# Cosine attention and a gated product on one core: pair 0's turned half copied earlier, the first tile of the second product parted at pass 12, one unit's loads behind a gather

## The chip, the cores and the metric

One Trainium2 chip, of which the kernel uses one core. The metric is the device time of one execution in microseconds (us), the median over several runs. Engines are named as in the profile: PE (TensorE, the matmuls), ACT (ScalarE), DVE (VectorE), POOL (GpSimd, which also issues the loads that convert f32 to bf16) and SP (SyncE, which here only issues DMAs).

## The reference

Inputs are q, k, v of 8 batches x 12 heads x 448 rows x 64 columns, and two weight matrices, 768 x 2048 and 2048 x 768. Cut to what is computed:

```
q_n = q / |q|;  k_n = k / |k|                      # along the 64 columns
attn = softmax(q_n @ k_n.T / 0.1)                  # 448 x 448 for each head
x    = (attn @ v) as a 3584 x 768 matrix           # rows: batch and row, columns: head and column
h    = x @ w_in;  g = h * cos(h)                   # 3584 x 2048
out  = g @ w_out                                   # 3584 x 768
```

## The kernel before, in words

**Pieces of work.** Two heads are a pair; 48 pairs are numbered 0 to 47, six to a batch. Three pairs are a unit; units 0 to 15, two to a batch. One batch's x is 448 columns of `xT`.

**What a pair goes through.** SP loads its k and q into `raw` (`load`, L586, DMAs at L589). They are squared (`square`, L618, on ACT at L627 or POOL at L629), DVE sums the squares (`reduce`, L632, L636), ACT turns the sum into a reciprocal root with a logarithm and an exponential (`rnorm`, L644, L657 and L660; for some units POOL does it, L653 and L654), and POOL or DVE scales q and k into `qks` (`scale`, L663, L668). `transposes` (L681) turns `qks` into `qkT`: for pairs 0 to 8 on PE (L692) with a DVE copy out of PSUM (L706), from pair 9 on by a transposing DMA of SP (L685). Pair 0 alone is handled in two parts a and b: four of the seven row blocks, then three; each has its own scaling, transposes and copy, and the two copies go from two PSUM tiles, `MP` and `AV`. `scores` (L709) makes four score blocks (block 0 is half as wide, L727; blocks 1 to 3, L719), each followed by ACT's exponential into `PX` (L734). Blocks alternate between PSUM banks, so a block also waits for whoever read the bank last. `attend` (L739) multiplies with v: R (the short block, L760), AV and S (L767, and L775, L783, L801 or L814 for the row sums).

**Sums of a unit.** For most pairs the products and the row sums leave PSUM undivided into `xu` (L847 on ACT, L850 on DVE). `chain` (L884) then does a unit at a time: SP gathers the row sums (`gather`, two DMAs at L888, pieces of 21 values of four bytes), DVE adds and inverts them (`sum` at L900, `recip` at L903), SP writes them to DRAM (`spread`, L904) and reads them back broadcast into `RB` (`bcast`, L906), and POOL multiplies into `xT` (L910). Other pairs are divided directly.

**The two products.** `m1` (L925, matmuls at L918) makes h of one batch in 8 groups of two 128-row tiles, n = 0 to 15. Each group fills one PSUM bank, ACT takes the cosine (L947), DVE multiplies into `gT` (L949, group 0 to 7), and three banks go round, so group 6 (n 12 and 13) fills the bank that group 3 filled, group 7 (n 14 and 15) that of group 4. `m2` makes out in tiles of 128 rows from `gT` and `W2`, with 16 passes for each of two column halves; it is poured into the pairs' stream piece by piece, so PE has work while other engines prepare. While pairs run it goes as `m2_quarters` (L998, matmuls at L1016, four 64 x 64 matmuls a pass and half, DVE copies out at L983). In tile 0 the passes are parted: passes 0 to 7 of both halves, then 8 to 15 of both, since the last `gT` groups and the last quarter of W2 come late. At the start of each part, PE waits until the part before has drained (`settled`, L143).

**What sets the order.** PE's order is the order in which the program is written: `pair` (L1188) and its numbers `given` and `six` (how many passes of m2 go behind each of the four score blocks), and for later pairs a text, `script`, in which `s46.0` is a score block, `f12` is 12 passes of m2, and `a45`, `b45`, `c45` are the three stages of `attend`. Only the first stretch, up to the first full product, is free within a window, and matmuls on zeros (`filler`, L1075) fill its holes. For ACT, DVE, POOL and SP, `arrange` (L153) plays the program with written costs and gives each operation a due time; the most urgent of the ready ones goes next, and that order is fixed in the program. So a changed due time or a changed belief of when a DMA lands (`pad`; `late` for the gathers, `LATE` for loads of v) changes orders far away, too. `order_only(first, then)` (L140) puts one operation behind another on the same engine; `queue` lists such pairs. Each engine runs its own list strictly in order.

Work around unit 6's gather: the first product of batch 2 (pairs 12 to 17, M1 2.0 to 2.15) runs while unit 6 (pairs 18 to 20) waits for its sums, and while k and q of units 8 and 9 are loaded. Pair 22 comes after it.

Of the kernel before, what the change touches and what calls it, by code (L numbers as in the profile page):

```python
# [13 lines left out]
PLAN = {  # L14
    "apart": 1,
    "ahead": (1, 2),
    "hurry": {},
    "rush": {},
    "swapped": {},
    "script": {19: """  # L20
        s19.0 f5 s19.1 f4 s19.2 f6 s19.3 f6 a18 f4 b18 s20.0 c18 c19
        s20.1 f2 a19 f2 b19 s20.2 f4 s20.3 f4 a20 s21.0 f4 s21.1 f4 b20 c20 s21.2 f6 s21.3 f6 o201 m2 c21
# [9 lines left out]
        s37.3 f4 s38.0 f4 s38.1 f4 s38.2 f4 s38.3 f4 a37 f2 b37 s39.0 c37 c38 s39.1 a38 f3 b38 f1 s39.2 f3 s39.3 f3 m5 c39  # L32
        a39 f4 s40.0 b39 f4 s40.1 f4 s40.2 f2 s40.3 f2 s41.0 s41.1 f4 s41.2 f5 s41.3 f5 a40 f2 b40 s42.0 c40 c41
        s42.1 a41 f3 b41 f1 s42.2 f4 s42.3 f4 s43.0 f4 s43.1 f4 s43.2 f5 s43.3 f5 a42 f2 b42 s44.0 c42 c43
        s44.1 f2 a43 f2 b43 s44.2 f5 s44.3 f7 a44 s45.0 f5 s45.1 f5 s45.2 f6 b44 c44 s45.3 f10 o012 m6 f6 s46.0 f12 a45 s46.1 b45 f4 c45 s46.2 f3 s46.3 f4
        """},
    "after": (0, 1, 2, 0, 1, 2, 0, 1),
    "queue": (("bcast13", "out18"), ("bcast9", "out11"), ("bcast11", "out15"),
              ("spread13", "T46"), ("spread9", "T34"), ("spread11", "T40")),
    "last": ((0,), (1,), (2,)),  # L40
    "folded": (0, 1, 2, 3),
    "grid": {2: (16, 5, 6), 3: (11, 3, 4), 4: (8, 2, 3)},
# [6 lines left out]
    "v3": (7, ("xa", 2, 0)),  # L49
    "late4": {2: (7, "T9")},  # L50
    "power": (2,),
    "late": 0.5,
    "mixed": (3, (3, 0, 1, 2, 0, 1, 2, 0), (2, 3, 4, 0, 1, 5)),
    "turned": 9,
    "first": (3, 1, 2, 0, 3, 1, 2, 0),
    "inner": {6: (6, 7), 7: (8,)},
    "other": (),
    "bs": -1.0,
    "cut": 8,
    "bx": 0.0,  # L60
    "six": (0, 8, 4, 4),
    "cycle": {13: 3, 14: 3, 15: 3, 16: 3, 17: 3, 18: 3, 46: 3, 47: 3},
# [7 lines left out]
    "u5": ("gather2", "gather2", "gather2"),  # L70
    "tail": 192,
    "twin": 4,
    "given": {13:(0,0,2,3),16: (4, 0, 5, 2), 22:(1,2,5,6), 34: (12, 4, 5, 6), 46: (12, 4, 3, 4), 47: (4, 0, 5, 0)},
    "roots": (3, (14, 0), (10, 0)),
    "lead": {33: 5, 45: 6, 12: 13, 21: 13},
    "vloads": {3: [(4, "x6"), (5, "x6")], 4: [(6, "x11")], 5: [], 6: [(7, "x15"), (8, "x15")]},
# [338 lines left out]
def bass_cosine_attention__then__act_gcu_kernel(  # L415
# [29 lines left out]
    LATE = 2.5  # L445
# [74 lines left out]
    P = Program(new_sem)  # L520
# [7 lines left out]
    def dma(eng, fns, reads, writes, sem, bulk=0.0, label="", behind=None, weight=1.0, pad=0.0):  # L528
        took, descs = 0.75, 0
        for y in ISSUE if eng == "SP" else ():  # L530
            if label.startswith(y):
                took, descs = ISSUE[y]
        o = P.op(eng, lambda e: [f(e) for f in fns], reads, writes, cost=took * len(fns), dma=sem, bulk=bulk, label=label)
        o.nd, o.descs, o.lead = len(fns), descs * len(fns), 0.3 if label[0] == "T" else 0.0
        o.weight, o.pad = weight, pad
        if behind is not None:
            P.order_only(behind, o)
        return o
# [19 lines left out]
    def dve(fn, reads, writes, cycles, lock=False, label="", bias=0.0):  # L558
        return P.op("DVE", fn, reads, writes, cost=0.15 + cycles / 960.0, lock=lock, label=label, bias=bias)

    def pool(fn, reads, writes, cost, label="", bias=0.0):
        return P.op("POOL", fn, reads, writes, cost=cost, lock=True, label=label, bias=bias)
# [35 lines left out]
    def load_v(u, behind=None, reads=()):  # L598
        if u >= NU:
            return  # L600
        i = u % 3
        b, hb = u // 2, UH * (u % 2)
        dma("POOL", [lambda e, z=z: e.dma_start(  # L603
            vav[i][BP * z : BP * z + BP, :, 1 - z : NT3 + 2 - z, :].rearrange("p h x d -> p h (x d)"),
            bass.AP(v.tensor, (b * NH + hb) * S * D + NT3 * D * z, [[NB * D, BP], [S * D, UH], [1, (NT3 + 1) * D]]))
            for z in range(2)],
            list(reads), [("va", i)], "va%d" % i, 2.67, "load v u%d" % u, behind,
            pad=LATE if u > 1 else 0.0)

    def halves(parts):  # L610
        if len(parts) == 1:
# [272 lines left out]
    def chain(u):  # L884
        i, b = u % 2, u // 2
        n = sum(UP * u + p not in PLAN["direct"] for p in range(UP))
        w = SPR // UP * n
        dma("SP", [lambda e, r=r: e.dma_start(  # L888
            sums[i].ap()[:, w * r : w * r + w],
            bass.AP(xu, (32 * r * 5 + 3 + i) * UP * S, [[64 * 5 * UP * S, 2], [w, 64], [1, w]]))  # L890
            for r in range(2)], [("xs", i, p) for p in range(n)], [("sums", i)], "sums%d" % i, 0.7,
            "gather%d" % u, pad=0.0 if u in PLAN["power"] else PLAN["late"])
        r = rcp[i].ap()[:, 0:w]
        parts = sums[i].ap()[:, 0 : 2 * w].rearrange("p (r x) -> p r x", r=2)
        if u in PLAN["power"]:
            pool(lambda e: e.tensor_tensor(r, parts[:, 0], parts[:, 1], ALU.add), [("sums", i)], [("rcp", i)], 0.23, label="sum")
            pool(lambda e: e.tensor_tensor(r, r, bass.AP(cst, 2, [[4, 128], [0, w]]), ALU.pow), [("rcp", i), "cst2"], [("rcp", i)],
                 0.05 + 0.166 * w, label="recip")
        else:
            dve(lambda e: e.tensor_reduce(out=r, in_=sums[i].ap()[:, 0 : 2 * w].rearrange("p (r x) -> p x r", r=2),  # L900
                                          axis=mybir.AxisListType.X, op=ALU.add), [("sums", i)], [("rcp", i)], 2 * w,
                label="sum", bias=PLAN["rush"].get(u, 0.0))
            dve(lambda e: e.reciprocal(r, r), [("rcp", i)], [("rcp", i)], 8 * w, label="recip", bias=PLAN["rush"].get(u, 0.0))  # L903
        dma("SP", [lambda e: e.dma_start(bass.AP(scr, u * UH * S, [[w, 128], [1, w]]), r)],  # L904
            [("rcp", i)], [("scr", u)], "scr", 0.02, "spread%d" % u).bias = PLAN["hurry"].get(u, 0.0)
        dma("SP", [lambda e, a=a: e.dma_start(  # L906
            RBv[i][64 * a : 64 * a + 64, 0:n], bass.AP(scr, u * UH * S + a * n * S, [[0, 64], [1, n * S]])) for a in range(2)],
            [("scr", u)], [("RB", i, p) for p in range(n)], "RB%d" % i, 3.4 * n / UP, "bcast%d" % u, None, 2.4, 0.5).bias = PLAN["hurry"].get(u, 0.0)
        for p in range(n):
            pool(lambda e, p=p: e.tensor_tensor(xTv[b % 2][:, UP * i + p, :], xuv[:, u % 3, p, :], RBv[i][:, p, :], ALU.mult),  # L910
                 [("RB", i, p), ("xa", u % 3, p)], [("xT", b % 2, UP * i + p)], 1.1, label="x%d" % (UP * u + p))
# [81 lines left out]
    def gates(t, f, m):  # L993
        par = sorted({(x // S) % 2 for x in (128 * t, 128 * t + 127)})
        return (sorted({("W2", y // 4) for y in range(f, f + m)})
                + sorted({("gT", x, y // 2) for y in range(f, f + m) for x in par}))
# [33 lines left out]
    def m2_fill(n, quarters=False):  # L1030
        while n > 0 and (m2_queue or m2_tile):
            if m2_tile or quarters and m2_queue[0][1:3] == [0, 0]:
                n -= m2_quarters(n)
                continue
            t, hf, f, bank, w = item = m2_queue[0]
            if bank is None:
                bank = item[3] = banks[0][nhalf[0] % len(banks[0])]
                nhalf[0] += 1
            name, po = bank
            col = (128 * t) % RING  # L1040
            m = min(4, n, NF - f)

            def go(e, po=po, f=f, m=m, col=col, w=w):
                for y in range(f, f + m):
                    r = e.matmul(po[:, 0 : w[1] - w[0]], gTv[:, y, col : col + 128], W2v[:, y, w[0] : w[1]],  # L1045
                                 start=(y == 0), stop=(y == NF - 1))
                return r

            P.op("PE", go, gates(t, f, m), name, cost=m * ((w[1] - w[0]) / 2400.0 + 0.0025), mode="F", label="M2 %d" % t)
            item[2] = f + m  # L1050
            n -= m
            if f + m == NF:
                m2_queue.pop(0)
                m2_drain(t, hf, name, po, w)
            elif f + m == NF - PLAN["twin"] and t == (B - 1) * S // 128 and not hf:
                m2_queue[0:2] = m2_queue[1::-1]
            elif f + m == NF - PLAN["twin"] and t == (B - 1) * S // 128:
                m2_queue[0:2] = m2_queue[1::-1]
# [21 lines left out]
    def find(label):  # L1080
        return [o for o in P.ops if o.label == label][-1]
# [106 lines left out]
    def pair(g, f):  # L1188
# [41 lines left out]
        if PLAN["v3"] and g == PLAN["v3"][0]:  # L1230
            load_v(3, None, [PLAN["v3"][1]])
# [10 lines left out]
    norms(0, 1)  # L1242
    first = ["first"]
    load_v(0, None, first)
    first = [("qks", 0, 0, 0)]
    load_w1(0, None, first)
# [55 lines left out]
    if not direct(NG - 1):  # L1302
        chain(NU - 1)
# [5 lines left out]
    banks[0] = [(["PO"], PO), (["TP"], TPF)] + [(BANKS.get(n, [n]), x[:, 0, :]) for n, x in PHs[:3]]  # L1309
    nhalf[0] = 0  # L1310
    m2_fill(10 ** 6)
    for x, y in PLAN["queue"]:
        P.order_only(find(x), find(y))
    P.arrange()
# [36 lines left out]
```

## Time and profile before

| | |
|---|---|
| median of 3 runs | 421.33 us (420.74 to 423.37) |
| the profiled execution's own time | 421.37 us |
| its span, first to last instruction | 419.6 us |
| around the span | 1.8 us |
| granted TensorE clock | 1.000 |
| PE busy | 410.8 us (98%) |
| ACT, POOL, DVE busy | 271.9, 242.7, 189.1 us |
| HBM traffic | 54.98 MB read, 11.13 MB written |

Times in the profile count from the first instruction. In a timeline, a line gives start, duration, engine, line of the kernel, operation, out<-in and shapes; the bracket is the idle time of the engine before it and what ended that. SPq and POOLq are DMA issues: their duration is the time to issue, not to land.

### The profile page before, as it was taken

To read this page: it belongs to the slowest core of one execution; us is meant where nothing else is said; L and a number is where in the kernel's file an instruction comes from. 1 tells how busy PE (TensorE), PEld (TensorE's weight loads), DVE (VectorE), ACT (ScalarE), POOL (GpSimd) and SP (SyncE) were. 2 spreads that over 40 slices of the span, in tenths; PEclk is the share of its full clock that TensorE was granted. 3 is DMA by queue.
4 is the path that set the end of the run, shared out by engine and by line. 5 is a ranking of instruction groups with operands and counts; after the bars stand their busy time and mean duration, and the time that the engine had idled before them with its cause. 6 is when DMAs were issued, how large, how long until landed. Compare 5 with 4: busy or idle time off the path is not lost.

```text
span 419.6 us, 13577 instructions
## 1 busy us (share of the span) xinstructions
PE 410.8 (98%) x6077; PEld 237.0 (56%) x6077; DVE 189.1 (45%) x250; ACT 271.9 (65%) x363; POOL 242.7 (58%) x193
## 2 busy tenths in 40 slices
PE   8899999999999999999999999999999999999997
PEld 3454556655556555665566555665566655565565
DVE  4564744456653277124752087213862244223421
ACT  5897578984986646877498556776498745703500
POOL 4999977989862694838864783908857320020000
PEclk9999999999999999999999999999999999999999
DMA  8999999979957998779867993969937720141023
GB/s 186 248 253 226 207 225 171 229 176 195 141 109 142 201 208 195 114 160 218 174 104 133 219 244 76 143 114 208 243 90 122 167 67 2 43 120 38 2 65 86
DMA packets 80254, 63.61 MB, mean 152 GB/s; under 512 B 44996, under 2 KB 75204, under 8 KB 80196
## 3 DMA queue, kind: packets, MB, share of 16 engines
q1 hardware_dynamic: 61988, 50.06, 56.8%
q0 software_dynamic: 18048, 12.59, 20.1%
q8 instruction: 48, 0.79, 0.8%
q10 hardware_dynamic: 160, 0.10, 0.1%
q14 instruction: 10, 0.08, 0.1%
HBM read 54.98 MB, written 11.13 MB: 158 GB/s over the span
## 4 chain that ended last, share of the span: by engine, by line
PE 84%; DMA 5%; ACT 4%; POOL 3%; DVE 2%; issue 1%; SPq 0%; ACTq 0%; DVEq 0%; POOLq 0%
PE MP L1016 25%; PE SC L918 18%; PE AV L918 10%; PE SC L719 6%; DMA sums<-xu 4%; PE AV L767 4%; PE MP L1045 4%; PE SC L1045 3%; PE AV L793 2%; ACT PX L734 2%; PE SC L767 2%; PE AV L760 2%; PE MP L918 2%; POOL qks L668 1%; ACT cosb L947 1%; DVE gT L949 1%
## 5 line engine op out<-in xcount | busy, mean ns | idle before, releaser
L734 ACT ACTIVATE PX<-SC 128x896 bf16<-128x896 f32 (+1 forms) x166 | 132.6, 828 | 25.5 <-PE SC L719 16.8
L1016 PE MATMUL MP<-W,gT 64*64 64x384 bf16 x2816 | 142.1, 323 | 0.9 <-DVE qkT L706 0.6
L1016 PEld LDWEIGHTS MP<-W,gT 64*64 64x64 bf16 x2816 | 79.0, 107 | 36.0 <-PE MP L1016 4.2
L668 POOL TENSOR_TENSOR qks<-raw,rn 128x896 bf16<-128x896 f32 (+1 forms) x48 | 79.8, 1678 | 28.5 <-ACT rn L660 27.9
L918 PE MATMUL SC<-xT,W 128*128 128x448 bf16 x468 | 94.9, 353 | 0.0
L947 ACT ACTIVATE cosb<-SC,cst 128x896 f32<-128x896 f32 x39 | 39.1, 1006 | 57.0 <-PE SC L918 55.1
L629 POOL TENSOR_TENSOR sq<-raw 128x896 bf16<-128x896 f32 x44 | 73.5, 1689 | 4.4 <-DMA raw<-in_q_dram 2.5
L910 POOL TENSOR_TENSOR xT<-xu,RB 128x448 bf16<-128x448 f32 x34 | 37.8, 1137 | 60.5 <-DMA RB<-scr 60.5
L918 PEld LDWEIGHTS SC<-xT,W 128*128 128x128 bf16 x468 | 45.5, 98 | 42.8 <-ACT xu L847 0.6
L949 DVE TENSOR_TENSOR gT<-SC,cosb 128x896 bf16<-128x896 f32 x39 | 42.3, 1088 | 37.5 <-ACT cosb L947 36.1
L918 PE MATMUL AV<-xT,W 128*128 128x448 bf16 x264 | 56.7, 353 | 0.0
L983 DVE COPY osb<-MP 128x384 f32<-128x384 f32 x50 | 25.7, 551 | 64.8 <-PE MP L1016 54.2
L636 DVE TENSOR_REDUCE n<-sq 128x14 f32<-128x896 bf16 (+2 forms) x49 | 51.2, 1057 | 5.9 <-ACT sq L627 5.2
L719 PE MATMUL SC<-qkT 64*64 64x448 bf16 x504 | 45.6, 356 | 0.6 <-ACT PX L734 0.4
L918 PEld LDWEIGHTS AV<-xT,W 128*128 128x128 bf16 x264 | 25.6, 98 | 24.2 <-ACT xu L847 0.3
L947 ACT ACTIVATE cosb<-AV,cst 128x896 f32<-128x896 f32 x22 | 22.1, 1006 | 23.6 <-PE AV L918 20.7
L949 DVE TENSOR_TENSOR gT<-AV,cosb 128x896 bf16<-128x896 f32 x22 | 23.9, 1087 | 15.2 <-ACT cosb L947 15.2
L603 POOL DMA_DIRECT2D va<-in_v_dram x32 | 21.9, 689 | 7.0 <-DMA raw<-in_q_dram 4.3
L877 POOL TENSOR_TENSOR xT<-xu,RB 128x448 bf16<-128x448 f32 x8 | 9.1, 1134 | 29.1 <-ACT RB L873 29.1
L850 DVE COPY xu<-AV 128x896 f32<-128x896 f32 x13 | 14.2, 1091 | 21.2 <-PE AV L783 14.3
L734 ACT ACTIVATE PX<-AV 128x896 bf16<-128x896 f32 (+1 forms) x26 | 21.1, 812 | 2.5 <-PE AV L719 1.7
L719 PEld LDWEIGHTS SC<-qkT 64*64 64x64 bf16 x504 | 14.5, 105 | 14.4 <-ACT PX L734 6.1
(95 smaller groups left out, 430.4 us busy)
## 6 DMA issues: line engine op xcount, KB each, us to landing
raw<-in_k_dram SPq DMA_DIRECT2D x48, 224.0 KB, 6.1
raw<-in_q_dram SPq DMA_DIRECT2D x48, 224.0 KB, 6.9
out_dram<-osb SPq DMA_DIRECT2D x54, 192.0 KB, 3.6
va<-in_v_dram POOLq DMA_DIRECT2D x32, 192.0 KB, 7.8
RB<-scr SPq DMA_DIRECT2D x18, 336.0 KB, 4.8
W<-in_moe_w_in_dram POOLq DMA_DIRECT2D x4, 768.0 KB, 14.7
W<-in_moe_w_out_dram POOLq DMA_DIRECT2D x4, 768.0 KB, 19.4
RB<-scr SPq DMA_DIRECT2D x6, 224.0 KB, 3.7
```

The source lines that it names most:

```text
L629: pool(lambda e, x=x, y=y: e.tensor_tensor(y, x, x, ALU.mult), src_, dst, 0.1 + n * 1.78e-3, label="sq%d.%d" % (u, p)).pad = LATE if u > 1 ...
L636: dve(lambda e, w=w: e.tensor_reduce(out=n2v[i][:, 2 * p : 2 * p + 2, w], in_=sqv[p][:, :, w, :], axis=mybir.AxisListType.X, op=ALU.add), ...
L668: f = lambda e, s0=s0, s1=s1: e.tensor_tensor(qksv[i][:, p, s0:s1].rearrange("p s h d -> p h s d"), rawv[i][:, h, s0:s1, :], bass.AP(rn[i] ...
L719: m = e.matmul(ph[BP * o : BP * o + BP, a, 0:S], t[r, c - 1 + (NT3 + 1) * o, 0:BP], t[r, :, BP : 2 * BP], start=True, stop=True)
L734: act(lambda e: e.activation(PHv[j] if c == 0 else PXv[j][:, c - 1], ph[:, :, 0:n], ACT.Exp, scale=1.0 / TAU), keys, [("PX", j, c)], 2 * n ...
L910: pool(lambda e, p=p: e.tensor_tensor(xTv[b % 2][:, UP * i + p, :], xuv[:, u % 3, p, :], RBv[i][:, p, :], ALU.mult), [("RB", i, p), ("xa", ...
L918: t = e.matmul(ph[:, a, 0:S], W1v[:, order[c], 128 * n : 128 * n + 128], xTv[b % 2][:, order[c], :], start=(c == 0), stop=(c == NKC - 1))
L947: act(lambda e, ph=ph, cz=cz: e.activation(cosv[cz], ph[:, :, 0:S], ACT.Sin, bias=cst.ap()[:, 0:1], scale=1.0), names(gi) + ["cst0"], [("c ...
L949: dve(lambda e, ph=ph, cz=cz, gi=gi: e.tensor_tensor(gTv[:, 2 * gi : 2 * gi + 2, S * (b % 2) : S * (b % 2) + S], ph[:, :, 0:S], cosv[cz], ...
L983: dve(lambda e: e.tensor_copy(dst, po[:, 0:n]), name, [("osb", o, hf)], n, label="osb%d" % t)
L1016: r = e.matmul(POH[b][x : x + 64, 0:HW], gTv[k, y, col + x : col + x + 64], W2v[k, y, HW * b : HW * b + HW], start=(y == 0 and h == 0), st ...
L1045: r = e.matmul(po[:, 0 : w[1] - w[0]], gTv[:, y, col : col + 128], W2v[:, y, w[0] : w[1]], start=(y == 0), stop=(y == NF - 1))
```

## The change

Named parts:

- **Opening.** A new `order_only` puts the second copy of pair 0's turned half (`qkT0`, part b) ahead of the sum of pair 2's squares (`red0.2`) on DVE.
- **Tile 0.** `cut` goes from 8 to 12: passes 0 to 11 of both halves, then 12 to 15 of both.
- **Unit 9's loads.** Three entries in `queue` put the loads of unit 9 behind unit 6's gather on SP.
- **Smaller ones.** The planner believes that the gathers of units 9, 11 and 13 land 1.0, 1.2 and 1.0 us later instead of 0.5 us later, and that v of units 2 and 3 lands 2.5 us sooner; pair 13 gets 3 and 2 passes of m2 behind its last two score blocks instead of 2 and 3; pair 45's first stage moves ahead of 12 passes of m2. `sum` gets the unit in its name, which changes no order by itself.

```
-  ... s45.3 f10 o012 m6 f6 s46.0 f12 a45 s46.1 b45 f4 c45 s46.2 f3 s46.3 f4
+  ... s45.3 f10 o012 m6 f6 s46.0 a45 f12 s46.1 b45 f4 c45 s46.2 f3 s46.3 f4
...
-              ("spread13", "T46"), ("spread9", "T34"), ("spread11", "T40")),
+              ("spread13", "T46"), ("spread9", "T34"), ("spread11", "T40"),
+              ("gather6", "load u9 p0"), ("gather6", "load u9 p1"), ("gather6", "load u9 p2")),
...
-    "late": 0.5,
+    "late": {9: 1.0, 11: 1.2, 13: 1.0},
...
-    "cut": 8,
+    "cut": 12,
...
-    "given": {13:(0,0,2,3), ...
+    "given": {13: (0, 0, 3, 2), ...
...
-            pad=LATE if u > 1 else 0.0)
+            pad=LATE if u > 3 else 0.0)
...
-            "gather%d" % u, pad=0.0 if u in PLAN["power"] else PLAN["late"])
+            "gather%d" % u, pad=0.0 if u in PLAN["power"] else PLAN["late"].get(u, 0.5))
...
     m2_fill(10 ** 6)
+    P.order_only(find("qkT0"), find("red0.2"))
     for x, y in PLAN["queue"]:
         P.order_only(find(x), find(y))
     P.arrange()
```

What this makes of the engines' lists, from the instruction order of the two programs:

- PE: 35 fillers instead of 38 in the first stretch; pair 0's block 2 ahead of pair 1's transposes; pair 2's block 2 ahead of pair 3's transposes, and similar moves of single blocks up to pair 5; the passes of tile 0; the two moves at pairs 13 and 45.
- ACT: pair 0's part b logarithm ahead of pair 1's squares; pair 2's logarithm behind two exponentials of pair 0 and its reciprocal root behind three (they stood ahead of all); unit 1's logarithms likewise one exponential later; one exponential of pair 22 ahead of unit 9's logarithm.
- DVE: the two copies of `qkT0` in a row, then `red0.2`; `sum` of unit 6 moves up, behind the third of unit 8's sums of squares and ahead of group 4 of M1 2, and unit 9's three sums of squares move down (`red9.0` behind group 6, `red9.1` and `red9.2` behind the copy of pair 21); `sum` of unit 10 moves ahead of `red13.1`; unit 11's `recip` moves behind two output copies; `red15.0` moves ahead of group 7 of M1 5.
- POOL: the third W1 load is issued with the second; the second and third W2 loads are issued ahead of v of unit 2; v of unit 15 goes behind unit 15's squares.
- SP: behind the transpose of pair 23 come the output of tile 5, then `gather6`, then unit 9's loads (before: the loads, `gather6`, the output).

More of the change, by code (lines that the diff above doesn't have):

```diff
@@ L34 @@
         s42.1 a41 f3 b41 f1 s42.2 f4 s42.3 f4 s43.0 f4 s43.1 f4 s43.2 f5 s43.3 f5 a42 f2 b42 s44.0 c42 c43
-        s44.1 f2 a43 f2 b43 s44.2 f5 s44.3 f7 a44 s45.0 f5 s45.1 f5 s45.2 f6 b44 c44 s45.3 f10 o012 m6 f6 s46.0 f12 a45 s46.1 b45 f4 c45 s46.2 f3 s46.3 f4
+        s44.1 f2 a43 f2 b43 s44.2 f5 s44.3 f7 a44 s45.0 f5 s45.1 f5 s45.2 f6 b44 c44 s45.3 f10 o012 m6 f6 s46.0 a45 f12 s46.1 b45 f4 c45 s46.2 f3 s46.3 f4
         """},
@@ L72 @@
     "twin": 4,
-    "given": {13:(0,0,2,3),16: (4, 0, 5, 2), 22:(1,2,5,6), 34: (12, 4, 5, 6), 46: (12, 4, 3, 4), 47: (4, 0, 5, 0)},
+    "given": {13: (0, 0, 3, 2), 16: (4, 0, 5, 2), 22:(1,2,5,6), 34: (12, 4, 5, 6), 46: (12, 4, 3, 4), 47: (4, 0, 5, 0)},
     "roots": (3, (14, 0), (10, 0)),
@@ L901, in chain @@
                                           axis=mybir.AxisListType.X, op=ALU.add), [("sums", i)], [("rcp", i)], 2 * w,
-                label="sum", bias=PLAN["rush"].get(u, 0.0))
+                label="sum%d" % u, bias=PLAN["rush"].get(u, 0.0))
             dve(lambda e: e.reciprocal(r, r), [("rcp", i)], [("rcp", i)], 8 * w, label="recip", bias=PLAN["rush"].get(u, 0.0))
```

## The prediction

> **What bounds the kernel now.** First the page: how busy is each engine.
>
> ```profile
> span 419.6 us, 13577 instructions
> PE 410.8 (98%) x6077; PEld 237.0 (56%) x6077; DVE 189.1 (45%) x250; ACT 271.9 (65%) x363; POOL 242.7 (58%) x193
> PEclk9999999999999999999999999999999999999999
> ```
>
> PE is idle for 8.8 us in all, and its matmul count in the products is not changed, so a gain must come out of those 8.8 us and out of the opening, where PE also counts fillers as busy. Next the waits of PE, in total:
>
> ```profile
> engine line waited for: us in total, times, longest us
> PE MP L1075 <- DVE zt L1074: 1.9, 1, 1.9
> PE MP L692 <- POOL qks L668: 0.7, 2, 0.6
> PE MP L1016 <- DVE qkT L706: 0.6, 1, 0.6
> PE AV L719 <- DVE gT L949: 0.6, 1, 0.6
> PE SC L727 <- ACT PX L734: 0.5, 1, 0.5
> PE SC L719 <- ACT PX L734: 0.4, 2, 0.2
> ```
>
> They sum to 4.7 us (a seventh row has 0.2): 1.9 before the first filler, 0.6 at 56.73 (tile 0 waits for the copy of pair 8), 0.6 at 165.56, the rest mostly in the opening. PE is busy for 20.55 of the last 23.57 us, and these 3.0 us of the tail are not touched. So hardly 1% (4.2 us) is there to be won. The wait at 165.56 has its cause on DVE:
>
> ```profile
> 154.86 1.08 DVE L636 TENSOR_REDUCE n<-sq 128x14 f32<-128x896 bf16 x1
> 156.12 1.09 DVE L949 TENSOR_TENSOR gT<-AV,cosb 128x896 bf16<-128x896 f32 x1 [0.18 <-ACT cosb L947]
> ...
> 161.96 0.20 DVE L900 TENSOR_REDUCE rcp<-sums 128x21 f32<-128x42 f32 x1 [2.48 <-DMA sums<-xu]
> ...
> 162.40 1.03 DVE L949 TENSOR_TENSOR gT<-SC,cosb 128x896 bf16<-128x896 f32 x1
> 163.34 1.07 DVE L636 TENSOR_REDUCE n<-sq 128x14 f32<-128x896 bf16 x1
> 164.33 1.08 DVE L949 TENSOR_TENSOR gT<-AV,cosb 128x896 bf16<-128x896 f32 x1
> ```
>
> The sum of unit 6 sits in DVE's list before groups 6 and 7 of M1 2 and waits for its gather to 161.96. Group 6's cosine was there at 160.63. Group 7 ends at 165.41, and pair 22's block 1 needs its bank. SP's timeline shows why the gather is late:
>
> ```profile
> 147.70 0.61 SPq L589 DMA_DIRECT2D raw<-in_q_dram  x1
> 148.40 3.58 SPq L888 DMA_DIRECT2D sums<-xu  x2
> 152.02 7.75 SPq L987 DMA_DIRECT2D out_dram<-osb  x4
> ```
>
> It is issued at 148.40 behind units 8's and 9's loads. By the trace's packet records its 256 packets of 84 bytes run only from 156.9 to 161.3.
>
> **Unit 9's loads behind the gather (the main term).** SP's transpose of pair 23 ends issue at 144.41. Then come tile 5's output (two DMAs, 1.23 us at an undisturbed place, 130.67) and the gather (1.17, as at 118.61); its last input, pair 20's copy on ACT, ends at 143.17, so SP does not wait. Unit 9's packets start at about 149.0 today; the output's 0.39 MB take some 2.3 us at the 172 KB/us that the loads move then (96 packets of 1792 bytes a us from 149 to 157), so the gather's packets start at about 151.3. They took 1.3 us at 120.0 and 4.4 us at 156.9 beside v's loads; 0.6 us to land. It lands at 153.2 to 156.3. Its sum now stands behind the sum of squares that ends at 155.94: no wait, or 0.4.
> Then DVE: group 6 at 160.66 to 161.75, unit 9's first sum of squares to 162.75, group 7 when its cosine is there (162.90): 162.93 to 164.02. PE's stream reaches pair 22's block 1 at 164.96 (24 matmuls end there). The 0.60 goes: **-0.6**. Next late is the transpose of pair 24, landed at 171.24 for 173.72; 1.9 us of cover remain. Between the ends 0 (the wait returns, below) and -0.6 I take -0.6, since 0.9 us of slack covers it.
> Queued behind: unit 9's loads, the two outputs, the spread. The squares of unit 9 ended at 159.44 and POOL then idled 5.74 us up to 165.18, so loads 2 to 5 us later are covered there.
>
> **Opening.** A DVE operation is put behind another here; no wait on another engine is added, but `red0.2` and what needs it come later. Today the second copy starts at 11.16 behind `red0.2` (10.15 to 11.24), and block 0 at 11.68, 0.17 after the copy ends at 11.51. Its transposes end at 10.62. Now: copy 10.67 to 11.02, block 0 at 11.19, **0.49 earlier**. `red0.2` moves to 10.94 to 12.03. ACT's logarithm now also stands behind blocks 0 and 1 (starting 0.34 after the matmul, 1.35 for both: to 12.88) and the reciprocal root behind block 2: 12.79, block 2 at 12.98, root 13.79 to 14.00. POOL starts 0.15 behind a root (7.25 to 7.40), so pair 2's scaling can start at 14.15; today POOL is free for it at 14.22: cover 0.07. The same count for unit 1's first root (its exponentials go on at 13.9, 14.7, 15.35 and 16.4) ends at 17.42, for a POOL free at 17.50: no cover.
>
> ```profile
> 10.93 1.74 POOL L668 TENSOR_TENSOR qks<-raw,rn 128x896 bf16<-128x896 f32 x1
> 12.58 1.72 POOL L629 TENSOR_TENSOR sq<-raw 128x896 bf16<-128x896 f32 x1
> 14.22 1.72 POOL L668 TENSOR_TENSOR qks<-raw,rn 128x896 bf16<-128x896 f32 x1
> 15.86 1.70 POOL L629 TENSOR_TENSOR sq<-raw 128x896 bf16<-128x896 f32 x1
> 17.50 1.71 POOL L668 TENSOR_TENSOR qks<-raw,rn 128x896 bf16<-128x896 f32 x1
> ```
>
> This unbroken POOL row, not pair 0, releases pair 3's transposes at 19.26, and from there PE has no hole above 0.13. So of the 0.49 only the PE work now done before 19.26 stays: pair 2's block 2, 0.25 us (eight matmuls take 0.50). Against it, pair 2's block 0 now stands before pair 0's second R and waits for the copy of 17.41: some 0.1. Between +0.3 (both covers fail) and -0.5 I take **-0.15**, near what the POOL row leaves.
> W1's third issue (0.88) now precedes pair 4's scaling: that ends at 24.3 instead of 23.39, its transposes run at 25.52: 1.2 cover, and pair 5's scaling is as before.
>
> **Tile 0 parted at 12.** Passes 8 to 11 now run at 58.30; group 5 is done at 51.87, and W2's third quarter, issued at 36.11 with the longest landing of 20.4, lands by 56.5. The fourth quarter (41.89 + 19.8 = 61.7) is needed later than before. v of unit 2, issued last, takes the third quarter's place: 56.5 for 59.81. The second boundary inside a run without a score block drains once more: the row shows 0.07 at 63.66, so **+0.1**.
>
> **Small ones, together -0.1.** Unit 11's inversion behind the copies frees PE's 0.11 at 277.68 (**-0.1**); its spread, 1 us later, has bcast 11 behind a transpose (278.95) anyway. Pair 13: same work, 0. Pair 45's R at 353.5: its bank is freed by 352.27 (group 6, 351.18 + 1.09), 0; else up to 1.0. Unit 10's sum and `red15.0` fill DVE idle time, 0; unit 10's gather is there before 254.27. Later belief of landings: 0 by itself.
>
> **Sum** against the profiled execution's own 421.37 (419.6 span, 1.8 around it, 0.04 above the median): -0.6 - 0.15 + 0.1 - 0.1 = **420.6**.
>
> **Rivals.** *The wait returns.* Unit 9's first squares come so late that `red9.0`, now ahead of group 7, holds it: group 7 must start by 163.8, so the load must land by 161.0. It lands at 153.72 today; with 2.3 for the output and 4.4 for the gather, 160.4. Beyond 161.0 each us costs one; at 161.6 all is as before: 421.2. For it: 0.6 us of margin only.
> [...]
> *The sum blocks DVE earlier (slower).* It now stands ahead of group 4. That group's bank is needed by n = 14 at 159.36, so a gather later than 159.36 - 1.09 - 0.29 = 157.98 stalls PE one for one. If it lands only with v of unit 8 (160.05), PE loses 2.1: 421.37 - 0.15 + 0.1 - 0.1 + 2.1 = 423.3. Against it: it stands before 768 packets of loads instead of behind them.
> [...]
> *The opening loses.* Both covers fail, +0.3 instead of -0.15, and the drains cost more: 421.1.
> *The change does not do what it says:* the lists show that it does; that it buys nothing is 421.3.
> *The opening keeps its 0.49:* 420.2.
>
> **Chances.** Forecast 0.50; wait returns 0.13; opening loses or nothing moves 0.17; opening keeps more 0.09; sum blocks DVE 0.07; something not seen, over 1% slower, 0.04. Of this, 1% (4.2 us) is about what a measurement can tell from no change: faster 0.02, same 0.93, slower 0.05. The range, 419.6 to 422.4, takes in both bounds of the opening and the first three rivals, leaving out the DVE block and the unseen; the spread of the runs before reaches from 420.74 to 423.37.
>
> **What would show it.** Right: the gather's sum starts by 156.5, group 7 ends near 164.0, no wait of PE on `gT`; pair 0's first block near 11.2, pair 3's transposes still near 19.3. Wrong: a new PE wait on `gT` near 159 to 161, a hole of POOL before 14.2 or 17.5, or any new PE wait above 0.5 after 57.

## The result, and the profile after

The changed kernel takes 420.7 us in the median (21 executions, 420.51 to 422.03), the kernel before 421.6 beside it (21 executions, 420.49 to 423.37 but for one of 704.35); the ratio is 0.9979 with a 95% interval of 0.997 to 0.9989. That is 0.9 us or 0.2%, inside the 1% that the text on record counts as no change, and 0.1 above the predicted 420.6.

The page of the changed kernel, the lines that answer to the first ones shown of before:

```profile
span 418.8 us, 13571 instructions
PE 409.6 (98%) x6074; PEld 236.5 (56%) x6074; DVE 189.5 (45%) x250; ACT 271.3 (65%) x363; POOL 242.7 (58%) x193
PEclk9999999999999999999999999999999999999999
```

PE is idle for 9.2 us now, 0.4 more than before, and yet the span is 0.8 shorter: three fillers (counted as busy) went, and the holes of the opening are plain idle time instead. The waits of PE:

```profile
PE MP L1076 <- DVE zt L1075: 1.9, 1, 1.9
PE MP L693 <- POOL qks L669: 1.6, 3, 0.7
PE MP L1017 <- DVE qkT L707: 0.6, 1, 0.6
PE SC L720 <- ACT PX L735: 0.6, 3, 0.2
PE SC L728 <- ACT rn L661: 0.4, 1, 0.4
PE SC L728 <- DVE qkT L707: 0.2, 1, 0.2
PE MP L1017 <- PE MP L1017: 0.2, 1, 0.2
PE MP L693 <- DVE qkT L707: 0.2, 1, 0.2
```

The row `AV L719 <- DVE gT` of before has gone and none on `gT` takes its place. In the opening the row on `qks` has grown from 0.7 to 1.6, one on `rn` is new, and the two rows on `PX`, 0.9 together, have become one of 0.6. A row is new in which PE waits for itself, in tile 0. DVE around the place of the old wait (a line's columns as before):

```profile
155.31 1.08 DVE L637 TENSOR_REDUCE n<-sq 128x14 f32<-128x896 bf16 x1
156.30 0.19 DVE L901 TENSOR_REDUCE rcp<-sums 128x21 f32<-128x42 f32 x1
156.57 1.09 DVE L950 TENSOR_TENSOR gT<-AV,cosb 128x896 bf16<-128x896 f32 x1
...
161.11 1.09 DVE L950 TENSOR_TENSOR gT<-SC,cosb 128x896 bf16<-128x896 f32 x1 [1.18 <-ACT cosb L948]
162.12 1.07 DVE L637 TENSOR_REDUCE n<-sq 128x14 f32<-128x896 bf16 x1
163.38 1.09 DVE L950 TENSOR_TENSOR gT<-AV,cosb 128x896 bf16<-128x896 f32 x1 [0.19 <-ACT cosb L948]
```

The sum starts at 156.30 with no bracket: it waits for nothing. Groups 6 and 7 are now held by their cosines. POOL squares unit 9's first load from 156.74, in time for the sum of squares at 162.12 ahead of group 7:

```profile
156.74 1.68 POOL L630 TENSOR_TENSOR sq<-raw 128x896 bf16<-128x896 f32 x1 [3.77 <-DMA raw<-in_q_dram]
```

SP's timeline has the output and the gather ahead of unit 9's loads:

```profile
144.44 1.23 SPq L988 DMA_DIRECT2D out_dram<-osb  x2
145.77 1.64 SPq L889 DMA_DIRECT2D sums<-xu  x2
147.45 3.60 SPq L590 DMA_DIRECT2D raw<-in_k_dram  x1
```

Where the 0.8 us of span comes from: the start of the same PE instruction in both traces, after minus before, at places along the stream.

| place | after minus before, us | step |
|---|---|---|
| pair 0's first block (11.68 before) | -0.98 | |
| pair 4's block 2 (29.78) | -0.01 | the opening's lead is gone |
| pair 8's block 1 (64.82), behind tile 0's parts | +0.33 | +0.35 |
| pair 14's products (114.48) | +0.45 | +0.1 |
| pair 22's block 1 (165.56) | -0.32 | -0.77 |
| first passes of tile 16 (277.68) | -0.62 | -0.3 |
| pair 46's block 1 (355.56) | -0.73 | -0.1 |
| end | -0.8 | |

### The profile page after: what moved, and what is told of

It is laid out like the page before. It is cut to its first block, busy times and chain, and to the rows that moved or that the text cites. A ratio compares the mean times of both kernels' runs of the same rounds, so it can differ in the third digit from the quotient of the medians.

```text
span 418.8 us, 13571 instructions
## 1 busy us (share of the span) xinstructions
PE 409.6 (98%) x6074; PEld 236.5 (56%) x6074; DVE 189.5 (45%) x250; ACT 271.3 (65%) x363; POOL 242.7 (58%) x193
## 4 chain that ended last, share of the span: by engine, by line
PE 92%; ACT 4%; POOL 1%; DVE 1%; DMA 1%; issue 1%; SPq 0%; ACTq 0%; POOLq 0%
PE MP L1017 27%; PE SC L919 21%; PE AV L919 11%; PE SC L720 6%; PE AV L768 4%; PE MP L1046 4%; PE SC L1046 3%; PE SC L768 2%; PE AV L761 2%; PE AV L794 2%; PE MP L919 2%; ACT PX L735 2%; PE SC L728 1%; ACT cosb L948 1%; PE MP L809 1%; PE AV L1046 1%
```

## The experiments

Unless a diff says otherwise, the lists of ACT, DVE, POOL and SP are those of the kernel that the edit starts from, and only what is shown moves; in the two runs on the opening they are arranged anew, and what else moves is said there. Ratios are to the kernel before, in executions on the same chip.

### The gather late again, with its sum

```
  SP:   T23  -out5  -gather6  load u9 p0, p1, p2  +gather6  +out5
  DVE:  g2.4, red9.0, g2.5, sum6, recip, g2.6, red9.1, g2.7    (as before)
```

> The changed kernel with one part undone: unit 6's gather again behind unit 9's loads, and the sum and unit 9's sums of squares at their old places on DVE; every other list as in the changed kernel. Theory (the late gather held DVE): the wait of PE on gT comes back before pair 22's block 1, 0.6 us, and all behind it is 0.6 to 0.75 us later than in the changed kernel; span 419.4 to 419.6, 421.3 beside the changed kernel's 420.7. Rival (the gain came from lighter traffic or from other work moved): the wait does not return, or under 0.2 us.

Measured: span 419.4, 421.03 us, ratio 0.9984 (0.9969 to 0.9999). The waits have the row of before back:

```profile
PE AV L720 <- DVE gT L950: 0.6, 1, 0.6
```

and DVE's sum is held by its gather again:

```profile
162.25 0.20 DVE L901 TENSOR_REDUCE rcp<-sums 128x21 f32<-128x42 f32 x1 [2.43 <-DMA sums<-xu]
```

Up to pair 22 PE stands 0.11 or less ahead of the changed kernel, from there 0.62 to 0.65 behind it to the end. So in the trace the main term is the late gather that holds DVE, and the rival of lighter traffic falls. The medians, over executions in which the stops and gathers of the sections below differ too, are 0.3 apart, and the interval overlaps that of the changed kernel (0.997 to 0.9989): by time alone the loss is not clear of noise.

### The gather late, its sum early: the slower rival made real

```
  SP:   T23  -out5  -gather6  load u9 p0, p1, p2  +gather6  +out5
```

> The changed kernel with only SP's part undone: the gather behind unit 9's loads again, but the sum still ahead of group 4 on DVE. This makes the slower rival of the prediction: a gather landing at about 162.0 against 157.98, from which PE loses one for one. Theory: a new wait of PE on gT near 159.4 of about 4.0 us, span about 422.8, time about 424.6. Rival (PE has other work for the free time, or the gather lands with the lighter load order by 158): under 0.5 us.

Measured: span 423.3, 425.08 us, ratio 1.0064 (1.0035 to 1.0094). The total is what was expected, the make-up is not. DVE's sum and PE's wait:

```profile
160.65 0.20 DVE L901 TENSOR_REDUCE rcp<-sums 128x21 f32<-128x42 f32 x1 [4.23 <-DMA sums<-xu]
162.00 3.38 PE L919 MATMUL AV<-xT,W 128*128 128x448 bf16 x12 [1.99 <-DVE gT L950]
```

The sum started at 160.65, not 162, and PE's wait was 2.0 us, not 4.0. The rule of the text on record, 1.09 + 0.29 from the sum's start to PE, gives 162.03, and PE went on at 162.00: so far the price of one for one was right. The rest is in this table of PE's busy time and granted clock (columns: window, its length, then busy us and instructions of PE, PEld, DVE, ACT, POOL, then PEclk, DMA share, GB/s):

```profile
160.00:162.00 2.00, 0.01 (x2) 0.04 (x2) 1.35 (x4) 0.12 (x1) 0.00 (x0) 1.00 0.78 294
162.00:163.00 1.00, 1.00 (x6) 0.54 (x7) 1.00 (x3) 0.89 (x1) 0.00 (x0) 1.00 0.14 40
163.00:164.00 1.00, 1.00 (x5) 0.42 (x4) 1.00 (x2) 0.00 (x0) 0.00 (x0) 0.66 0.04 4
164.00:165.00 1.00, 1.00 (x4) 0.30 (x2) 1.00 (x2) 0.00 (x0) 0.00 (x0) 0.50 0.01 5
165.00:166.00 1.00, 1.00 (x10) 0.30 (x12) 0.01 (x1) 0.53 (x1) 0.00 (x0) 0.50 1.03 339
166.00:167.00 1.00, 1.00 (x20) 0.36 (x16) 0.49 (x1) 0.98 (x2) 0.00 (x0) 0.63 0.96 220
167.00:168.00 1.00, 1.00 (x36) 0.77 (x36) 0.61 (x1) 0.99 (x2) 0.00 (x0) 1.00 0.60 124
```

1.3 us after PE resumes, its clock goes to 0.50, and stays there to about 166.7. PE's lag on the changed kernel grows from 2.18 us at 162.0 to 3.81 at 166.8 with no wait of its own. The wait cost 2.0 and the clock behind it another 1.6; 0.7 of the end's 4.5 is a stop at 320 (below). The clock does not fall every time: five of the nine executions have a mean granted clock of 0.995 or 0.996 and took 425.08 to 427.1 us, the other four have 1.000 and took 422.18 to 423.3, which is 1.5 to 2.6 above the changed kernel's median, about the wait. The rival's place, sign and price of the wait were right; what it left out is the clock.

### The gather's part alone, on the kernel before

```
  SP:   T23  +out5  +gather6  load u9 p0, p1, p2  -gather6  -out5
  DVE:  sum6, g2.4, recip, g2.5, g2.6, red9.0, g2.7, xu21, red9.1    (as in the changed kernel)
```

> The kernel before with this one part done: output of tile 5 and unit 6's gather ahead of unit 9's loads, the sum ahead of group 4, unit 9's sums of squares down; nothing else moved. Theory: the wait of 0.6 on gT at 165.56 goes, 0.6 to 0.75 us gained from there to the end: span 418.85 to 419.0, about 420.7, that is nearly the whole of the change's gain. Rival (the gain in the changed kernel needs the other parts too): 0.3 us or less.

Measured: span 419.7, 421.38 us, ratio 0.9998 (0.9982 to 1.0014): no gain that can be measured. Yet at pair 22 PE came 0.94 earlier than in the kernel before, and only 0.17 of that it had already at 150. It lost 0.35 of the lead near 277 and 0.75 near 324.5, where PE waits 0.47 and 0.56 (the kernel before: 0.11 and nothing) for the output copies of DVE. These stand behind the sum of a unit (11, 13) that started 4.9 and 5.6 us after the issue of its gather. So the gain at 165 is there in this trace too, and what becomes of it is decided by two gathers further on. The next three runs are about those.

### Unit 11's inversion

```
  DVE:  sum11  +recip  osb15 osb15  -recip  xu37
```

> The changed kernel with unit 11's inversion back ahead of the two output copies on DVE; nothing else moved. In the changed kernel its sum starts at 274.19, before the copies can (275.97). Theory A (the prediction's term: the inversion held the copies, so its place gained the time at 277.68): a wait of PE on the copies of 0.3 to 0.45 us comes back near 277. Theory B (the gather decides: it landed 2.85 us after issue in the changed kernel, 4.55 in the kernel before): with a gather that lands by 275 nothing is lost, 0 us and span 418.8; only with one that lands 4.5 us after issue is 0.3 lost.

Measured: span 418.7, 420.93 us, ratio 0.9989 (0.998 to 0.9997); PE within 0.1 of the changed kernel everywhere behind the opening, no wait near 277. Theory A falls: with a gather as early as this one (2.85 us) the place of the inversion is worth nothing, so it was not what gained 0.3 at 277.68. The two traces show what was. Kernel before:

```profile
276.23 0.20 DVE L900 TENSOR_REDUCE rcp<-sums 128x21 f32<-128x42 f32 x1 [4.63 <-DMA sums<-xu]
276.47 0.29 DVE L903 RECIPROCAL rcp<-rcp 128x21 f32<-128x21 f32 x1
276.67 0.95 DVE L983 COPY osb<-MP 128x384 f32<-128x384 f32 x2
```

Changed kernel:

```profile
274.19 0.20 DVE L901 TENSOR_REDUCE rcp<-sums 128x21 f32<-128x42 f32 x1 [2.92 <-DMA sums<-xu]
275.97 1.02 DVE L984 COPY osb<-MP 128x384 f32<-128x384 f32 x2 [1.59 <-PE MP L1017]
```

In the first, the sum waits for its gather to 276.23 and the copies come behind it; in the second the gather is there 2 us sooner and the copies wait for PE alone.

### The gather's part with the inversion moved

```
  the edit of the run before last, and
  DVE:  sum11  -recip  osb15 osb15  +recip  xu37    (on the kernel before)
```

> The kernel before with the gather's part and the inversion of unit 11 behind the output copies; nothing else. With the gather's part alone the span was 419.7: 0.94 won at 165.56, then 0.47 lost near 277 (copies behind unit 11's sum and inversion) and 0.56 near 324.5 (copies behind unit 13's sum, whose gather landed 5.6 us after issue, 3.25 in the kernel before). Theory: the wait near 277 is 0.1 or gone; the one near 324.5 hangs on that gather alone: gone if it lands within 3.5 us (span 418.8 to 419.0), 0.5 again if it takes over 5 (span 419.3). Rival (both waits come from PE being early, whatever the copies wait for): both waits as with the gather's part alone, 419.7.

Measured: span 419.2, 421.4 us, ratio 1.0 (0.9989 to 1.0012). No wait near 277 (the sum of unit 11 started 2.86 us after the issue of its gather), 0.27 at 324.07 (that of unit 13 after 5.17), and 0.35 lost near 114. The rival falls, since one of the two waits is gone. Whether a gather lands early decides, and that differs between executions whose lists agree around it: 2.85 us for unit 11 in the changed kernel, 4.60 in the run below that changes only the opening.

### What held a gather: a 16 KB instruction fetch

In the packet records, the gather of unit 11 sends its last packet 2.36 to 2.38 us after the issue, in three executions where the sum started early and four where it started late; only its completion differs. The gather's semaphore says so directly: the counts of its second DMA come 2.82 and 2.83 us after the issue in the changed kernel, 4.50 and 4.53 in the kernel before, so it is not DVE that is late. What else differs is a packet of 16 KB on the profile's instruction queue (48 of them in every execution, one for some 253 of the changed kernel's 12,148 matmuls and weight loads, and by that count taken here for PE's own), which took 0.9 to 2.6 us. Time after the gather's issue at which that fetch began and at which the sum started, in us (the sum was held by the gather alone; the version at the end, whose sum of unit 11 stands behind copies, is left out of unit 11's rows):

| gather | fetch begins | sum starts | executions |
|---|---|---|---|
| unit 9 | 1.90 to 2.65 | 4.19 to 5.05 | 10 |
| unit 9 | 3.08 to 3.17 | 2.85 to 3.00 | 4 |
| unit 11 | 2.43 to 2.57 | 4.55 to 5.15 | 5 |
| unit 11 | 2.79 to 3.07 | 2.85 to 2.86 | 8 |

Where the fetch began up to 2.65 us after the issue, the sum started 0.5 to 0.9 us after the fetch's own end; where it began at 2.79 or later, the sum did not wait for its end. The changed kernel is in the last row (3.05), the kernel before in the one above it (2.48). To test this rather than argue it, the fetch was moved: 34 more PE instructions ahead of it.

```
- P.filler = (lambda e, shut: e.matmul(PO[:, 0:S], zt.ap()[:, 0:128], zt.ap(), start=shut, stop=shut), zero, MM, 0.3)
+ P.filler = (lambda e, shut: parted(e, shut, PO, zt, S), zero, MM, 0.3)    # first 17 fillers: two halves
  and  DVE:  sum11  +recip  osb15 osb15  -recip  xu37
```

> The kernel with unit 11's inversion ahead of the copies (which alone lost nothing, its gather having landed at 2.85 us), and with the first 17 fillers of the opening each made of two matmuls of half the columns: 34 more PE instructions (matmul and weight load), the same columns. Theory (PE's instruction fetch holds the gather): the trace has 48 fetches of 16 KB for PE's 12,132 instructions, one for some 253; near 270 to 275 they follow each other in 4.2 us, so 34 instructions move each by about 0.55 us ahead. The fetch that began 3.05 us after the issue of unit 11's gather comes at about 2.5, as in the executions where the sum started 4.5 to 5.2 us after the issue: the sum at 4.4 to 4.9, a wait of PE of 0.3 to 0.45 us on the copies near 277. Rival (the landing is chance, or set by the transpose behind it alone): the sum at 2.85 and no wait.

Measured: 421.33 us, ratio 0.9993 (0.998 to 1.0007); span 421.2 in the profiled execution, 419.0 to 421.2 in all. The fetch began 2.43 us after the issue, the sum started at 4.77, and PE waited 0.33 near 279:

```profile
278.02 0.20 DVE L901 TENSOR_REDUCE rcp<-sums 128x21 f32<-128x42 f32 x1 [4.85 <-DMA sums<-xu]
278.25 0.29 DVE L904 RECIPROCAL rcp<-rcp 128x21 f32<-128x21 f32 x1
278.46 0.95 DVE L984 COPY osb<-MP 128x384 f32<-128x384 f32 x2
```

All three numbers are as the theory had them; the rival falls. What it did not foresee is 1.9 us lost in the opening of the profiled execution: v of unit 0 landed at 17.66, PE stood for 0.94 until 17.70, and its clock was 0.50 from about 18.3 to 21.7 (columns as above):

```profile
17.00:18.00 1.00, 0.30 (x8) 0.22 (x8) 0.62 (x2) 0.96 (x3) 1.00 (x2) 1.00 1.19 257
18.00:19.00 1.00, 1.00 (x16) 0.41 (x16) 0.58 (x1) 0.55 (x1) 1.00 (x1) 0.65 1.26 281
20.00:21.00 1.00, 1.00 (x13) 0.21 (x10) 0.28 (x1) 0.76 (x3) 1.00 (x2) 0.50 1.28 222
```

Its mean clock is 0.996; the other nine executions have 0.999 or 1.000.

### Tile 0 parted at 8 again

```
-    "cut": 12,
+    "cut": 8,
```

> The changed kernel with tile 0 parted at pass 8 again, the lists of ACT, DVE, POOL and SP kept as in the changed kernel. Theory (the parting at 12 has one boundary more that no score block covers, and each such boundary drains PE): PE comes 0.3 us earlier from pair 8's block 1 on and keeps it to the end: span 418.5, 0.3 under the changed kernel. By the prediction's term it would be 0.1. Rival (the loss at tile 0 came from late W2 or late groups, not from the boundary): a wait at passes 8 to 11 on W2 or gT, and nothing gained or a loss.

Measured: span 418.3, 420.51 us, ratio 0.9972 (0.9959 to 0.9986). PE in tile 0, changed kernel:

```profile
62.97 0.66 PE L1017 MATMUL MP<-W,gT 64*64 64x384 bf16 x12
63.80 0.68 PE L1017 MATMUL MP<-W,gT 64*64 64x384 bf16 x12 [0.16 <-PE MP L1017]
64.28 0.29 PE L728 MATMUL SC<-qkT 64*64 64x224 bf16 x4
64.38 0.95 PE L1017 MATMUL MP<-W,gT 64*64 64x384 bf16 x12
65.15 0.36 PE L720 MATMUL SC<-qkT 64*64 64x448 bf16 x4
```

Parted at 8:

```profile
62.95 1.41 PE L1017 MATMUL MP<-W,gT 64*64 64x384 bf16 x24
64.19 0.27 PE L728 MATMUL SC<-qkT 64*64 64x224 bf16 x4
64.29 0.66 PE L1017 MATMUL MP<-W,gT 64*64 64x384 bf16 x12
64.78 0.36 PE L720 MATMUL SC<-qkT 64*64 64x448 bf16 x4
```

The same 24 and 12 matmuls take 1.24 and 0.49 us from start to next block with the parting at 8, 1.31 and 0.77 with that at 12. The boundary at pass 24 stands inside the 24 in both kernels, that at 28 inside the 12 only in the changed one: 4 matmuls, a drain, 8 matmuls. It costs 0.28. PE is 0.38 ahead at pair 8's block 1 and 0.5 at the end, where 0.1 comes from a stop near 114 that this execution does not have. The median is 0.2 under the changed kernel's, with overlapping intervals. No wait for W2 or for a group shows with either, so the rival falls.

### The opening

Two runs: the order of pair 0's copies taken back, and the copies kept but pair 0's second R put ahead of pair 2's block 0.

```
-    P.order_only(find("qkT0"), find("red0.2"))
```

> The changed kernel without the order of the two copies of pair 0 (the opening's lists of all engines fall back to those of the kernel before; W1's third issue goes back behind pair 4's squares, and W2's loads stay as in the changed kernel). Theory: block 0 comes 1 us later, but PE reaches pair 4's block 2 at the same time, since pair 2's block 0 now holds pair 0's second R up to 17.33 and POOL's row releases pair 3's transposes at 19.23 either way: span 418.7 to 418.9, no loss. By the prediction's term it would be 419.0 (0.15 lost), if the opening kept its lead 419.3 to 419.8.

```
     P.order_only(find("qkT0"), find("red0.2"))
+    P.order_only(find("R0"), find("SC2.0"))
```

> The changed kernel with one order more on PE: pair 0's second R ahead of pair 2's block 0 (as in the kernel before), the copies still in a row. Theory (the lead was lost at that block, which waits for a copy to 17.33): R at about 16.9, the row sums' end at 18.2 in place of 18.68, pair 0's broadcast near 19.1 in place of 19.57, and a part of 0.4 us kept at pair 4's block 2. Rival (POOL's unbroken row sets the opening's end, whatever PE does before): R comes earlier, but pair 4's block 2 stays at 29.77 within 0.1, and the span at 418.8.

Measured: 421.61 us, ratio 0.9995 (0.9981 to 1.0009), span 419.9; and 421.24 us, 0.9995 (0.9985 to 1.0005), span 420.3. Both spans hold stops of PE far away (next run): 1.0 us near 316 in the first, 1.0 near 114 in the second, so the opening is read at its own end. In the first run all lists of the opening are those of the kernel before; in the second they are so from 17.9 to the opening's end:

| kernel | v of unit 0 lands | pair 0's block 0 | its second R | pair 3's transposes | pair 4's block 0 | pair 4's block 2 |
|---|---|---|---|---|---|---|
| before | 15.97 | 11.68 | 17.41 | 19.26 | 27.59 | 29.78 |
| changed | 15.56 | 10.70 | 17.42 | 19.23 | 27.41 | 29.77 |
| parted at 8 | 16.98 | 10.83 | 17.40 | 19.21 | 27.38 | 29.74 |
| copies' order back | 16.91 | 11.83 | 17.42 | 19.30 | 27.59 | 29.79 |
| R first | 17.11 | 10.95 | 17.52 | 19.21 | 27.69 | 29.88 |
| fillers halved | 17.66 | 10.63 | 18.07 | 20.98 | 29.34 | 31.70 |

Block 0 comes a whole microsecond sooner or later and pair 4's block 2 stays within 0.11 of the changed kernel's, but for the last row, in which PE is late by its own clock. Pair 3's transposes say where the lead goes. They start some 0.05 behind the end of POOL's scaling of pair 3, which is 19.17 in the changed kernel and 19.21 in the kernel before:

```profile
17.46 1.71 POOL L669 TENSOR_TENSOR qks<-raw,rn 128x896 bf16<-128x896 f32 x1
```

One block of pair 2 is done ahead of that in the changed kernel, so PE reaches pair 4's block 0 at 27.41 for 27.59 with the same matmuls done. Up to block 2 this 0.18 goes too: the same 43 matmuls, in another order, take 2.36 us in place of 2.19, and neither trace shows idle time there. Why that order takes longer is not shown.

The rival of the second run is right in its outcome: putting R first gains nothing, and POOL's row stands where it stood. But the run does not tell what an earlier R would bring, since R came no earlier in it:

```profile
17.15 0.28 PE L761 MATMUL AV<-PX,va 64*64 64x224 bf16 x2 [0.34 <-DMA va<-in_v_dram]
17.16 0.28 PE L761 MATMUL AV<-PX,ones 64*64 64x224 bf16 x2
17.52 0.28 PE L761 MATMUL AV<-PX,va 64*64 64x224 bf16 x2
```

The first R waits for v of unit 0, which landed at 17.11 in this execution, and the second stands 0.37 behind it. In the changed kernel's profile v was there early (15.56), and there the hole before pair 2's block 0 (row `SC L728 <- ACT rn`, 0.4) brought the second R to 17.42. What stays open: by its medians the kernel with the copies' order back is 0.7 us behind the one with the inversion moved, on the same chip, although its opening ends at the same time; the intervals of the two overlap, and these runs do not tell whether more than the stops and the held gathers is behind it.

### Pair 13's passes, pair 45's first stage

```
-    13: (0, 0, 3, 2)
+    13: (0, 0, 2, 3)
```

> The changed kernel with pair 13's passes 2 and 3 in place of 3 and 2; nothing else. The prediction's term was 0, but PE loses up to 0.4 us near 114 in the changed kernel against the kernel before. Theory (a stop of PE near 114 goes with the fetch of instructions, not with the passes): the passes change nothing by themselves; a loss near 114 is there only if the fetch before it begins less than about 3.3 us ahead. Rival (the place of the passes costs it): 0.1 to 0.4 us gained there with the old numbers.

Measured: span 419.3, 421.22 us in one execution: 0.5 slower than the changed kernel's 420.7, by a stop at 114.5 that the profile ends on nothing but "issue":

```profile
113.83 0.26 PE L728 MATMUL SC<-qkT 64*64 64x224 bf16 x1
114.51 0.29 PE L728 MATMUL SC<-qkT 64*64 64x224 bf16 x3 [0.43 <-issue]
```

PE stops between the first and second of four matmuls of one block, which wait for the same inputs. In the 14 profiled executions such stops are near 114 and near 316 to 320, and behind the opening nowhere else above 0.2. In what follows a stop is the time that PE takes for the same matmuls around the place, above the shortest of the 14. Near 114 it was 0.36 to 0.96 us in the four executions whose 16 KB fetch began 1.9 to 2.1 us before pair 15's block 0 was due, and 0 to 0.26 in the ten in which it began 2.2 to 3.9 before; near 316, 0.73 and 1.04 in the two in which it began 1.3 us before pair 41's R, and nothing in the twelve in which it began 2.2 or more before. That a late fetch makes the stop is read from these 14; no run moved that fetch alone. The +0.1 at 109 to 115 in the changed kernel is a short stop at this place (0.18) less some 0.05 that the passes' new place gains ahead of it; the passes' place shows no loss.

```
-  s46.0 a45 f12 s46.1
+  s46.0 f12 a45 s46.1
```

> The changed kernel with pair 45's first stage again behind its 12 passes; nothing else. The prediction's term was 0. Theory: PE's start of pair 46's block 1 moves by 0.1 us or less and the end with it. Rival (the profiles of the two kernels differ by 0.1 to 0.2 us from there on): 0.1 to 0.2 us later, span 418.9 to 419.0.

Measured: span 418.9, 420.72 us in one execution; from 354 on PE is 0.15 to 0.17 later, and no earlier difference is above 0.01. So in this trace the move of pair 45's first stage gains 0.15, where the text on record had 0; one execution of each does not show it in the time.

### A version from what was found

```
-    "cut": 12,
+    "cut": 8,
  DVE:  -sum11  osb15 osb15  +sum11  recip
```

> The changed kernel with tile 0 parted at 8 and unit 11's sum, with its inversion, behind both output copies of tile 15, so that no copy waits for that gather. Theory: the 0.45 us of the parting at 8 stays and PE never waits near 277, wherever the gather lands: span 418.3 to 418.4, about 420.4. Rival (what is queued behind the sum): the spread goes out some 0.9 us later, behind it the transpose of pair 40 and the broadcast; the products x33 to x35 end near 288.7 in place of 287.8, while the first group of M1 5 reads the last of them from 289.4: with more than 0.7 us lost on the way PE waits there, up to 0.5 us.

Measured: 420.62 us (419.99 to 421.04), ratio 0.9969 (0.9955 to 0.9984), span 418.7 with a stop of 0.45 near 114 in it. No wait near 277, none in M1 5: the rival falls. It is faster than the kernel before and by its ratio 0.1% faster than the changed one, with overlapping intervals; the same holds of the parting at 8 alone (0.9972).

## Why the prediction was right, and which steps were not

The forecast of 420.6 against 420.7 is right in its total, sign and main term, and partly by terms that cancel. That the sum fits so closely is in part luck: 0.3 of the gain came from a gather that no edit aims at, and it makes up for an opening that gained nothing and a drain priced too low. The figures below are of single traces. The medians bear them out only in part: with the gather late again the ratio is 0.9984, with the opening's order back 0.9995, with the gather's part alone 0.9998, and all three intervals overlap that of the changed kernel. How much of the 0.9 us each part is worth on average is not shown.

- **Unit 9's loads behind the gather (-0.6).** Right in place and mechanism: -0.77 between the traces, and 0.7 lost at the same place when undone. The gather's sum started at 156.30 (within 156.5), group 7 ran at 163.38 to 164.47 (162.93 to 164.02 forecast; PE as a whole was 0.45 later there). Unit 9's first load was squared from 156.74, not 160.4: the step that added the whole 4.4 us of gather and 2.3 of output to its landing was too pessimistic, so the rival of the returning wait never came near.
- **Opening (-0.15).** Wrong step: "from there PE has no hole above 0.13. So of the 0.49 only the PE work now done before 19.26 stays." POOL's row released pair 3's transposes at 19.23, as the text had it, and 0.18 of PE's work stayed ahead up to 27.41. Behind that it was lost as well, in busy time and not in a hole, and at 29.77 nothing is left. Block 0 came 0.98 earlier, twice the forecast: part b's transposes ended at 10.25 and not 10.62, with fewer fillers ahead of them, so the copy started at 10.29 and not 10.67.
- **Tile 0 parted at 12 (+0.1).** Mis-sized: 0.28 for the boundary, 0.35 with what lies around it. It was priced by the row of 0.07 before the passes at 63.66, which is the idle time that the profile shows; the drain lies mostly inside the busy time of the group (0.95 us for 12 matmuls in place of 0.66).
- **Small ones (-0.1).** The term "Unit 11's inversion behind the copies frees PE's 0.11" is wrong in its cause: with the gather as early as it was, the inversion put back loses nothing. The 0.3 there came with a gather that was complete 1.7 us earlier, for a reason that no edit aims at. Pair 45's 0 was 0.15.
- **The slower rival.** Its place is shown by the run that made it, and so is its price for the wait. It was kept off because the gather stood ahead of the loads, as the text argued; what its price left out is the clock, which fell in five of nine executions.

## What to carry to other kernels

Look at a DMA's place in its queue and not only at its need: unit 6's gather, issued at 145.77 ahead of unit 9's loads in place of 148.40 behind them, let DVE's sum start at 156.30 in place of 161.96. So try such a DMA ahead of bulk loads, and the waiting instruction behind work that PE needs soon (with the gather late, PE waited 0.6 us with the sum there and 2.0 with the sum ahead). Follow the shift of PE to the end of the trace before adding terms: of the 0.94 gained at pair 22 by the gather's part alone, 0.35 went near 277 and 0.75 near 324.5, behind gathers whose sums started 4.9 and 5.6 us after the issue. An early operation can bring little: pair 0's copies had block 0 start 0.98 earlier and pair 4's block 2 0.01, as pair 3's transposes were released by POOL's unbroken row, which stayed at 19.2.

## What the runs showed of the hardware

- **After a wait of 2 us PE's granted clock was halved for over 3 us.** Behind a hole of 1.99 us the granted clock was 0.50 from about 163.3 to 166.7, and PE's lag grew by 1.6 us beside the 2.0; the mean clock was 0.995 or 0.996 in five of the nine executions and 1.000 in the other four. In the opening of the kernel with halved fillers the clock was 0.50 from about 18.3 to 21.7 in the profiled execution, behind a stand of 0.94 up to 17.70; PE's lag grew from 0.64 to 1.93, and of the ten executions this one alone has a mean clock under 0.999. How long a hole has to be, and what else it takes, is not shown.
- **A 16 KB instruction fetch went with stops of PE and with late gathers.** Stops of 0.36 to 0.96 us near 114 and of 0.73 and 1.04 near 316 came where such a fetch began 1.9 to 2.1 and 1.3 us ahead of the place, and of 0.26 at the most where it began 2.2 or more ahead. The sum behind a gather started 4.19 to 5.15 us after the gather's issue where a fetch began 1.90 to 2.65 after it, and 2.85 to 3.00 where it began 2.79 to 3.17 after it. With the fetch moved to 2.43 the sum started at 4.77; in the changed kernel they stand at 3.05 and 2.85.
- **A drain between two parts of one bank's passes cost 0.28 us in tile 0,** of which the profile shows 0.16 or less as idle time.
